# Two heads per block: a chunked linear-attention kernel with a token MLP, rewritten to work on pairs of heads

## The chip, the cores and the metric

The kernel runs on one core of a Trainium2 chip. A core has five engines with instruction streams of their own: PE (matrix products, into the accumulator memory PSUM), DVE (elementwise work, reductions, copies), ACT (functions such as Ln and Exp, and copies), POOL (elementwise work in SBUF, building of constants) and SP, which here only issues transfers. The metric is the time on the device, in microseconds (us). Before the change it is 325.19 us, the median of three runs (324.52 to 325.39).

## The reference

Inputs r, k, v, w have the shape [4 batches, 8 heads, 768 steps, 48]; w lies between 0.80 and 0.95. Each head carries a 48x48 state through the steps:

```python
for t in range(S):
    cur = einsum('bhd,bhe->bhde', u[None] * kt, vt)
    y[:, :, t] = einsum('bhd,bhde->bhe', rt, state + cur)
    state = wt[:, :, :, None] * state + einsum('bhd,bhe->bhde', kt, vt)
```

The heads' outputs are put side by side to x [4, 768, 384]. A token mixer without softmax follows, with weights w_q, w_k [384, 64] and w_out [384, 384]:

```python
W_tok = einsum('bsd,btd->bst', x @ w_q, x @ w_k) / sqrt(64)
out = maximum(einsum('bst,btd->bsd', W_tok, x), 0) @ w_out
```

## The kernel before, in words

Time is cut into 6 chunks of 128 steps. Within a chunk the recurrence becomes matrix products: the running product of w is taken as Exp of a running sum of Ln w (a product with a triangular matrix), r and k are scaled by it (r by the decay up to the step before, k by its inverse), and the chunk's output is a masked 128x128 product A of those two, times v, plus the scaled r times the state. The term with u touches only the diagonal; it is the row sum of u k r times v (VdB).

**Preparation** (lines 116 to 183) loops over the 8 heads of a batch. Four loads of two heads each (k and w on ACT's queue, r and v on SP's, two buffers) feed it. For each head ACT takes Ln (line 135), PE makes two running sums cw0 and cw1 (151, 152), ACT takes Exp of both (156, 157), DVE and POOL scale r and k into one tile, comb (160, 161), PE transposes it (165), DVE and ACT copy the two halves out of PSUM (167, 168), PE makes A in two groups of three chunks (175) and DVE masks it (176). POOL and DVE make the diagonal term (139 to 146). The last row of the decay is taken with products against a unit vector (182) and inverted (183).

**The scan** (185 to 201) loops over the 6 chunks, with all 8 heads in one PSUM tile: Y8 takes for each head AmB times v (128 rows) and r times the state (48 rows), in turn; DVE adds the diagonal term. Sn8 is k times v; DVE adds the state and POOL multiplies by the chunk's decay: the next state.

**The MLP** (203 to 247) transposes X, makes x w_q and x w_k in transposed form, transposes the latter, contracts over time first (Tps, 64x384), then over the 64 (mps, with a Relu), then with w_out (fps), and stores.

All is traced as one straight program. A planner puts each engine's instructions into one order when the kernel is built: it plays the program with its own estimates of cost and gives an engine, whenever it is free, the ready instruction that is earliest in the program text. On the chip each engine then keeps to that order. Tiles come from pools; a tag in a pool has a fixed number of buffers (`bufs`). In PSUM, which has eight banks, tag "big" (Y8, cw0, cw1, psumT) has four buffers and tag "p" (all others) has three:

```python
cw0 = ps.tile([C, NCH, D], F32, name="cw0", tag="big", bufs=4)
A = ps.tile([C, NCH // 2, C], F32, name="A", tag="p", bufs=3)
Y8 = ps.tile([C, H, D], F32, name="Y8", tag="big", bufs=4)
```

All matrix products are issued by a helper at line 52, so the profile shows them under L52 with their tiles' names.

## Time and profile before

| What | Value |
|---|---|
| Median of three runs | 325.19 us |
| Span of the profiled execution | 321.2 us, so about 4 us of a run's time lie outside the span |
| PE busy | 198.6 us, 1,480 products |
| ACT busy | 185.7 us, 290 instructions |
| DVE busy | 130.2 us, 300 instructions |
| POOL busy | 99.8 us, 141 instructions |
| Transfers | 24.3 MB in all, 64 loads of 288 KB and 24 stores of 192 KB |

A row of the groups names line, engine, operation, tiles written and read, shapes and count; then busy time and mean nanoseconds of one, then the idle time of the engine just before them and what ended it. In a row of the timeline come the start, the length and how many instructions of a kind were merged; the lengths of products contain a pipeline's end, so that the distance between starts is the measure of PE's pace. A row of the waits gives who waited for whom, the sum, how often, and the longest. The clock line gives the rate granted to PE in tenths.

### The profile page before, as it was taken

To read this page: it belongs to the slowest core of one execution; us is meant where nothing else is said; L and a number is where in the kernel's file an instruction comes from. 1 tells how busy PE (TensorE), PEld (TensorE's weight loads), DVE (VectorE), ACT (ScalarE), POOL (GpSimd) and SP (SyncE) were. 2 spreads that over 40 slices of the span, in tenths; PEclk is the share of its full clock that TensorE was granted. 3 is DMA by queue.
4 is the path that set the end of the run, shared out by engine and by line. 5 is a ranking of instruction groups with operands and counts; after the bars stand their busy time and mean duration, and the time that the engine had idled before them with its cause. 6 is when DMAs were issued, how large, how long until landed. Compare 5 with 4: busy or idle time off the path is not lost.

```text
span 321.2 us, 4038 instructions
## 1 busy us (share of the span) xinstructions
PE 198.6 (62%) x1480; PEld 126.9 (40%) x1480; DVE 130.2 (41%) x300; ACT 185.7 (58%) x290; POOL 99.8 (31%) x141
## 2 busy tenths in 40 slices
PE   0010453568996654499977654578975643599973
PEld 0000232346662333276642332366642332366631
DVE  0011555355411575563311754454320753653303
ACT  4634688870449978950579786950479574310350
POOL 1344324426311415453303115444303105103200
PEclk9999999999996855555576755555588555555589
DMA  9996454450014397530104762540104250000003
GB/s 154 184 197 130 87 105 82 77 108 2 0 39 73 93 223 127 111 73 2 38 0 76 194 139 44 105 73 2 37 0 76 92 129 1 1 2 2 1 0 147
DMA packets 104006, 24.30 MB, mean 76 GB/s; under 512 B 100529, under 2 KB 103986, under 8 KB 103986
## 3 DMA queue, kind: packets, MB, share of 16 engines
q1 hardware_dynamic: 53522, 14.26, 21.7%
q10 hardware_dynamic: 49664, 9.44, 16.6%
q0 software_dynamic: 800, 0.34, 0.8%
q8 instruction: 11, 0.18, 0.2%
q14 instruction: 9, 0.07, 0.1%
HBM read 19.66 MB, written 4.72 MB: 76 GB/s over the span
## 4 chain that ended last, share of the span: by engine, by line
PE 32%; issue 18%; ACT 17%; POOL 13%; DMA 11%; DVE 6%; SPq 2%; ACTq 0%; POOLq 0%; DVEq 0%
PE Y L52 15%; DMA vG<-in_v_dram 7%; POOL uk L139 4%; POOL urk L143 4%; POOL cbB L161 4%; ACT emcw L157 3%; ACT L156 3%; PE psumT L52 3%; PE wqk_ps L52 3%; ACT Kdc L168 3%; PE xt_ps L52 3%; DMA out_dram<-osb 2%; DVE osb L246 2%; DMA kG<-in_k_dram 2%; PE fps L52 2%
## 5 line engine op out<-in xcount | busy, mean ns | idle before, releaser
L161 POOL TENSOR_TENSOR cbB<-kG,emcw 128x288 bf16<-128x288 f32 x32 | 24.7, 772 | 112.6 <-ACT emcw L157 112.6
L52 PE MATMUL psumT<-ID,cbB 128*128 128x128 bf16 x192 | 25.5, 297 | 50.5 <-POOL cbB L161 38.4
L52 PE MATMUL A<-RdB,Kdc 48*128 48x128 bf16 x192 | 26.5, 298 | 38.6 <-ACT Kdc L168 32.0
L52 PEld LDWEIGHTS <-cbB 128*48 128x48 bf16 (+1 forms) x384 | 26.1, 130 | 58.0 <-POOL cbB L161 53.9
L52 PE MATMUL Y<-SB,RdB 48*128 48x48 bf16 x192 | 41.8, 218 | 3.5 <-POOL SB L200 3.5
L176 DVE TENSOR_TENSOR AmB<-A,US 128x384 bf16<-128x384 f32 x64 | 32.7, 551 | 26.5 <-PE A L52 26.1
L52 PE MATMUL Y<-VbB,AmB 128*128 128x48 bf16 x192 | 41.6, 223 | 0.0
L157 ACT ACTIVATE emcw<-cw,bias_mi 128x288 bf16<-128x288 f32 x32 | 15.9, 498 | 43.0 <-PE cw L52 42.8
L139 POOL TENSOR_TENSOR uk<-kG,ubc 128x288 f32<-128x288 f32 x32 | 25.2, 808 | 45.3 <-DMA kG<-in_k_dram 37.6
L135 ACT ACT_TABLE_LOAD x29 | 37.2, 1283 | 0.5
L52 PEld LDWEIGHTS <-Kdc 48*128 48x128 bf16 x192 | 17.7, 129 | 49.0 <-ACT Kdc L168 41.6
L168 ACT COPY Kdc<-psumT 48x768 bf16<-48x768 bf16 x32 | 25.5, 796 | 12.8 <-DVE RdB L167 12.2
L200 POOL TENSOR_TENSOR SB<-Ss,ptB 48x384 bf16<-48x384 f32 x24 | 20.5, 854 | 35.5 <-DVE Ss L198 35.5
L145 DVE TENSOR_REDUCE diag<-urk 128x6 f32<-128x288 f32 x32 | 14.2, 450 | 39.5 <-POOL urk L143 39.4
L167 DVE COPY RdB<-psumT 48x768 bf16<-48x768 bf16 x32 | 17.4, 544 | 27.4 <-PE psumT L52 27.4
L192 DVE TENSOR_TENSOR X<-Y,VdB 128x384 bf16<-128x384 f32 x24 | 13.3, 555 | 37.4 <-PE Y L52 37.4
L160 DVE TENSOR_TENSOR cbB<-rG,ecwx 128x288 bf16<-128x288 f32 x32 | 15.2, 474 | 30.5 <-ACT ecwx L156 30.0
L156 ACT ACT_TABLE_LOAD x20 | 25.7, 1283 | 1.3 <-ACT logw L135 0.9
L143 POOL TENSOR_TENSOR urk<-uk,rG 128x288 f32<-128x288 f32 x32 | 25.0, 799 | 1.1 <-DMA rG<-in_r_dram 1.0
L52 PEld LDWEIGHTS <-AmB 128*128 128x128 bf16 x192 | 20.1, 107 | 12.5 <-issue 3.9
L208 ACT COPY XT<-xt_ps 128x384 bf16<-128x384 bf16 x24 | 10.3, 483 | 25.1 <-PE xt_ps L52 25.1
L52 PEld LDWEIGHTS <-RdB 48*128 48x128 bf16 x192 | 19.4, 101 | 12.7 <-issue 3.3
(56 smaller groups left out, 283.8 us busy)
## 6 DMA issues: line engine op xcount, KB each, us to landing
kG<-in_k_dram ACTq DMA_DIRECT2D x16, 288.0 KB, 3.9
wG<-in_w_dram ACTq DMA_DIRECT2D x16, 288.0 KB, 4.0
rG<-in_r_dram SPq DMA_DIRECT2D x16, 288.0 KB, 3.6
vG<-in_v_dram SPq DMA_DIRECT2D x16, 288.0 KB, 4.3
out_dram<-osb SPq DMA_DIRECT2D x24, 192.0 KB, 2.0
wout_sb<-in_moe_w_out_dram POOLq DMA_DIRECT2D x1, 288.0 KB, 7.3
wq_f<-in_moe_w_q_dram SPq DMA_DIRECT2D x1, 96.0 KB, 3.8
wk_sb<-in_moe_w_k_dram POOLq DMA_DIRECT2D x1, 48.0 KB, 5.9
```

The lines of the kernel that those rows point to most:

```text
L52: nc.tensor.matmul(o, l, rr, start=start, stop=stop, skip_group_check=sgc, is_transpose=trans)
L135: nc.scalar.activation(logw, wS, ACT.Ln, bias=0.0, scale=LN_SCALE)
L139: nc.gpsimd.tensor_tensor(uk, kS, _rep(ubc[:, ds(h * D, D)], 1, NCH), ALU.mult)
L143: nc.gpsimd.tensor_tensor(urk, uk, rS, ALU.mult)
L156: nc.scalar.activation(ecwx, cw1, ACT.Exp, bias=bias_px, scale=1.0)
L157: nc.scalar.activation(emcw, cw0, ACT.Exp, bias=bias_mi, scale=-1.0)
L160: nc.vector.tensor_tensor(comb[:, :, 0:D], rS, ecwx, ALU.mult)
L161: nc.gpsimd.tensor_tensor(comb[:, :, 64:64 + D], kS, emcw, ALU.mult)
L167: nc.vector.tensor_copy(RdB[:, h], psumT[0:D])
L168: nc.scalar.copy(Kdc, psumT[64:64 + D])
L176: nc.vector.tensor_tensor(AmB[:, h, ds(g * (NCH // 2), NCH // 2)], A, MASKrep, ALU.mult)
L200: nc.gpsimd.tensor_tensor(SB2, Ss, _rep(ptB[:, :, c], 2, D), ALU.mult)
```

## The change

Four things change together.

Heads are worked on in pairs. Tiles with 128 columns hold head one in columns 0 to 47 and head two in columns 64 to 111; the columns between are set to zero once, in standing buffers (three each for logw and Rd, two for Kd and for the decay pt). One transpose then covers two heads, and r and k are transposed apart, both copied out by one DVE instruction (RKT). Exp and the mask work over two PSUM banks at once. A is made per head from partitions 0 to 47 and 64 to 111 of RKT.

The state is kept as one [128, 384] tile. The product of padded k and v of a pair gives a block per head on the diagonal and unwanted blocks beside it; the decay tile pt is zero there, so that the multiplication clears them. The old state is added in PSUM by a product with the identity, and one DVE multiplication makes the new state. The products of r with the state cover two heads each. The last chunk makes no state. The decay comes from products of logw with a column of ones (tile ptp, held over the whole preparation of a batch) and an Exp at its end.

One table set that holds Ln and Exp is named for ACT at the start. All loads are issued on SP's queue, w first, with three buffers; the weights of the MLP are loaded after the first batch's preparation in the text.

In the MLP x w_k is made directly with time on the partitions, two chunks of X are transposed into one PSUM tile, and the Vd product is given to POOL. PSUM is shared out anew: cw, psT and A have one buffer of two banks each, and all other tiles (ptp, Sn, Y8, xt_ps, wkps, wq_ps, Tps, mps, fps) share tag "m" with two buffers of one bank.

The diff, cut to its core (of the lines taken away, most are in the kernel above):

```diff
+    nc.scalar.preload_act_table_set("natural_log_exp_and_others")
...
+    ones = U128[:, C - 1:C]
...
+    nc.gpsimd.memset(bias_c, MU * C)
+    NB = 3
...
+    for i in range(NB):
+        t = consts.tile([C, NCH, C], BF16, name=f"logw{i}", tag=f"logw{i}")
+        nc.gpsimd.memset(t, 0.0)
+        LW.append(t)
+        t = consts.tile([C, NCH, C], BF16, name=f"RdS{i}", tag=f"RdS{i}")
+        nc.gpsimd.memset(t, 0.0)
+        RdS.append(t)
...
+    for i in range(2):
+        t = consts.tile([C, NP, NCH, C], BF16, name=f"KdS{i}", tag=f"KdS{i}")
+        nc.vector.memset(t, 0.0)
+        KdS.append(t)
+        t = consts.tile([C, NCH, H], F32, name=f"pt{i}", tag=f"pt{i}")
+        nc.vector.memset(t, 0.0)
+        PT.append(t)
...
-    ld = ctx.enter_context(tc.tile_pool(name="ld", bufs=2))
+    ld = ctx.enter_context(tc.tile_pool(name="ld", bufs=3))
...
+    def mtile(shape, dtype, name):
+        return ps.tile(shape, dtype, name=name, tag="m", bufs=2)
+
+    def prep(b, hp, AmB, RKT, VB, Vd, ptp):
+        n = b * NP + hp
...
+        for ap, tl in ((w, wG), (k, kG), (r, rG), (v, vG)):
+            nc.sync.dma_start(out=tl, in_=ap[b, ds(hp * 2, 2)].rearrange(
+                "h (c p) d -> p (h c) d", p=C))
+        if n == 0:
+            nc.sync.dma_start(out=u1, in_=u.rearrange("h d -> (h d)"))
+            nc.gpsimd.partition_broadcast(ubc, u1)
...
+        logw = LW[n % NB]
+        for hh in range(2):
+            nc.scalar.activation(logw[:, :, ds(hh * 64, D)],
+                                 wG[:, ds(hh * NCH, NCH)], ACT.Ln,
+                                 bias=0.0, scale=LN_SCALE)
+        cw1 = ps.tile([C, 2, 512], F32, name="cw1", tag="cw")
+        for hh in range(2):
+            mm(cw1[:, hh, 0:NCH * D], US128, logw[:, :, ds(hh * 64, D)])
+        ecwx = hw.tile([C, 2, NCH, D], BF16, name="ecwx", tag="ecwx")
+        nc.scalar.activation(ecwx.rearrange("p h c d -> p h (c d)"),
+                             cw1[:, :, 0:NCH * D], ACT.Exp,
+                             bias=bias_px, scale=1.0)
+        cw0 = ps.tile([C, 2, 512], F32, name="cw0", tag="cw")
...
+        for c in range(NCH):
+            mm(ptp[:, hp, ds(c, 1)], logw[:, c], ones)
+
+        Rd = RdS[n % NB]
+        Kd = KdS[b % 2][:, hp]
+        nc.vector.tensor_tensor(pad(Rd), chd(rG),
+                                ecwx.rearrange("p h c d -> p c h d"), ALU.mult)
+        nc.gpsimd.tensor_tensor(pad(Kd), chd(kG),
+                                emcw.rearrange("p h c d -> p c h d"), ALU.mult)
+        nc.scalar.copy(VB[:, :, ds(hp * 2, 2)], chd(vG))
+
+        psT = ps.tile([C, 2, 1024], BF16, name="psT", tag="psT")
+        for c in range(NCH):
+            mm(psT[:, 0, ds(c * C, C)], Rd[:, c], ID128, trans=True)
+        for c in range(NCH):
+            mm(psT[:, 1, ds(c * C, C)], Kd[:, c], ID128, trans=True)
+        nc.vector.tensor_copy(RKT[:, hp], psT[:, :, 0:NCH * C])
+
+        NG = NCH // 2
+        for g in range(2):
+            A = ps.tile([C, 2, 512], F32, name="A", tag="A")
+            for cc in range(NG):
+                c = g * NG + cc
+                for hh in range(2):
+                    mm(A[:, hh, ds(cc * C, C)],
+                       RKT[ds(hh * 64, D), hp, 1, ds(c * C, C)],
+                       RKT[ds(hh * 64, D), hp, 0, ds(c * C, C)])
+            nc.vector.tensor_tensor(
+                AmB[:, ds(hp * 2, 2), ds(g * NG, NG)],
...
+        nc.gpsimd.tensor_tensor(uk, hcd(kG), _rep(ubs, 2, NCH), ALU.mult)
+        nc.gpsimd.tensor_tensor(uk, uk, hcd(rG), ALU.mult)
+        diag = hw.tile([C, 2, NCH], F32, name="diag", tag="diag")
+        nc.vector.tensor_reduce(diag, uk, axis=AX.X, op=ALU.add)
+        nc.gpsimd.tensor_tensor(Vd[:, :, ds(hp * 2, 2)], VB[:, :, ds(hp * 2, 2)],
+                                _rep(diag.rearrange("p h c -> p c h"), 3, D),
+                                ALU.mult)
 
     for b in range(B):
...
+        ptp = mtile([C, NP, NCH], F32, "ptp")
+        for hp in range(NP):
+            prep(b, hp, AmB, RKT, VB, Vd, ptp)
+        for hh in range(2):
+            nc.scalar.activation(
+                pt.rearrange("p c (q h) -> p q c h", h=2)[ds(hh * 64, D), :, :, hh],
+                ptp[ds(hh * 64, D)], ACT.Exp, bias=bias_c[ds(hh * 64, D)],
+                scale=1.0)
...
+        for c in range(NCH):
+            if c + 1 < NCH:
+                Sn = mtile([C, DM], F32, "Sn")
+                if SB is not None:
+                    mm(Sn, ID128, SB, start=True, stop=False)
+                for hp in range(NP):
+                    mm(Sn[:, ds(hp * D2, D2)], KdS[b % 2][:, hp, c],
+                       VB[:, c, ds(hp * 2, 2)].rearrange("p h d -> p (h d)"),
+                       start=(SB is None and hp == 0), stop=True)
+                SB2 = sm.tile([C, DM], BF16, name="SB2", tag="SB")
+                nc.vector.tensor_tensor(
+                    SB2.rearrange("p (h d) -> p h d", d=D),
+                    Sn.rearrange("p (h d) -> p h d", d=D),
+                    _rep(pt[:, c], 2, D), ALU.mult)
+            Y8 = mtile([C, DM], F32, "Y8")
             for h in range(H):
...
+                mm(Y8[:, ds(h * D, D)], AmB[:, h, c], VB[:, c, h],
+                   start=(h == 0), stop=(c == 0))
+            if SB is not None:
+                for hp in range(NP):
+                    mm(Y8[:, ds(hp * D2, D2)], RKT[:, hp, 0, ds(c * C, C)],
+                       SB[:, ds(hp * D2, D2)], start=False, stop=True)
+            nc.vector.tensor_tensor(X[:, c], Y8,
+                                    Vd[:, c].rearrange("p h d -> p (h d)"), ALU.add)
...
+            if c % 2 == 1:
+                tp = mtile([128, NK, 2 * C], BF16, "xt_ps")
+                for cc in range(2):
+                    for dt in range(NK):
+                        mm(tp[:, dt, ds(cc * C, C)],
+                           X[:, c - 1 + cc, ds(dt * 128, 128)], ID128, trans=True)
+                nc.scalar.copy(XT[:, :, ds((c - 1) * C, 2 * C)], tp)
...
+        wkps = mtile([128, NCH, DH], F32, "wkps")
+        for c in range(NCH):
+            for kt in range(NK):
+                mm(wkps[:, c], XT[:, kt, ds(c * C, C)], wk_sb[:, kt],
+                   start=(c == 0 and kt == 0), stop=(kt == NK - 1))
+        nc.vector.tensor_copy(wk_s, wkps)
...
+        for n in range(2):
+            pp = mtile([DH, 384], F32, "wq_ps")
...
+        Tps = mtile([DH, DM], F32, "Tps")
...
+        for n in range(2):
+            for dt in range(NK):
+                mps = mtile([128, 384], F32, "mps")
...
         for c in range(NCH):
-            fps = ps.tile([128, DM], F32, name="fps", tag="p", bufs=3)
+            fps = mtile([128, DM], F32, "fps")
```

More of the change, by code (lines that the diff above doesn't have):

```diff
@@ L220 @@
[L220 to L229 removed]
+        for n in range(2):
+            pp = mtile([DH, 384], F32, "wq_ps")
+            for kt in range(NK):
+                mm(pp, wq_sb[:, kt], XT[:, kt, ds(n * 384, 384)],
+                   start=(kt == 0), stop=(kt == NK - 1))
+            nc.scalar.copy(wqT[:, ds(n * 384, 384)], pp)
```

170 lines of the change are left out of this document (48 added, 122 removed).

## The prediction

> **What bounds the kernel now.** I read the engines' totals and the granted clock first, then busy time by stage, the chain of waits, the groups by form and, for pitches, the timeline.
>
> ```profile
> span 321.2 us, 4038 instructions
> PE 198.6 (62%) x1480; PEld 126.9 (40%) x1480; DVE 130.2 (41%) x300; ACT 185.7 (58%) x290; POOL 99.8 (31%) x141
> PEclk9999999999996855555576755555588555555589
> ```
>
> No engine is full over the span, so the stages must differ. By stage (start:end, length, then busy time of PE, weight loads, DVE, ACT, POOL, granted clock, DMA share, GB/s):
>
> ```profile
> 40.00:75.00 35.00, 18.23 (x174) 13.19 (x175) 18.68 (x47) 26.76 (x35) 14.63 (x21) 1.00 0.46 86
> 75.00:92.00 17.00, 16.13 (x119) 11.10 (x119) 6.50 (x14) 5.20 (x10) 6.23 (x8) 1.00 0.09 17
> 92.00:112.00 20.00, 14.72 (x71) 7.06 (x69) 6.48 (x14) 17.46 (x29) 4.47 (x6) 0.83 0.29 60
> ```
>
> A batch has three stages. Preparation (40 to 75) is ACT's; the scan over chunks (75 to 92) is PE's, with ACT nearly idle; the token MLP (92 to 112) is ACT's again, because the next preparation runs beside it. From the chain of waits (start, us, what):
>
> ```profile
> 43.20 0.51 ACT emcw L157
> 43.78 0.73 POOL cbB L161
> ...
> 75.60 2.34 PE Y L52 x15
> ...
> 289.52 2.34 PE Y L52 x15
> ```
>
> A hand-over between engines costs about 0.07 us (43.71 to 43.78). The first scan is in full flow at 75.6, the fourth at 289.5: the period is 213.9/3 = 71.3 us, and 31.7 follow. The span is 75.6 + 3 x 71.3 + 31.7, and I forecast these three terms.
>
> **The change, engine by engine.** A "pair" is the two heads that the new preparation works on together; a batch has four.
>
> ```profile
> L135 ACT ACT_TABLE_LOAD x29 | 37.2, 1283 | 0.5
> L156 ACT ACT_TABLE_LOAD x20 | 25.7, 1283 | 1.3 <-ACT logw L135 0.9
> L157 ACT ACT_TABLE_LOAD x9 | 11.5, 1283 | 4.4 <-PE cw L52 4.3
> L157 ACT ACTIVATE emcw<-cw,bias_mi 128x288 bf16<-128x288 f32 x32 | 15.9, 498 | 43.0 <-PE cw L52 42.8
> L135 ACT ACTIVATE logw<-wG 128x288 bf16<-128x288 f32 x32 | 14.0, 442 | 1.3 <-DMA wG<-in_w_dram 0.9
> L168 ACT COPY Kdc<-psumT 48x768 bf16<-48x768 bf16 x32 | 25.5, 796 | 12.8 <-DVE RdB L167 12.2
> L161 POOL TENSOR_TENSOR cbB<-kG,emcw 128x288 bf16<-128x288 f32 x32 | 24.7, 772 | 112.6 <-ACT emcw L157 112.6
> L200 POOL TENSOR_TENSOR SB<-Ss,ptB 48x384 bf16<-48x384 f32 x24 | 20.5, 854 | 35.5 <-DVE Ss L198 35.5
> L114 POOL MEMSET SB<- 48x384 bf16 x4 | 1.7, 418 | 0.0
> L176 DVE TENSOR_TENSOR AmB<-A,US 128x384 bf16<-128x384 f32 x64 | 32.7, 551 | 26.5 <-PE A L52 26.1
> L145 DVE TENSOR_REDUCE diag<-urk 128x6 f32<-128x288 f32 x32 | 14.2, 450 | 39.5 <-POOL urk L143 39.4
> L167 DVE COPY RdB<-psumT 48x768 bf16<-48x768 bf16 x32 | 17.4, 544 | 27.4 <-PE psumT L52 27.4
> ```
>
> **ACT.** 58 table loads cost 74.4 us. One set for Ln and Exp removes them, and Kdc's 25.5 us moves into DVE's joint copy. From 288 to 768 elements ACT adds 298 ns, 0.62 an element, so one Exp over two banks and 576 elements is 0.50 + 0.18 = 0.68 us (at worst two old ones, 1.00). A pair: two Ln 0.88, two Exp 1.36, the V copy 0.62, together 2.9 us; with some 7 us of evacuations a batch is 19 against 46 now.
>
> **DVE.** 288 and 384 elements give 148 ns plus 1.05 an element. A pair: Rd 0.75, joint copy of 1,536 bf16 0.94 (the old copy's 0.52 an element), two masks of 768 at 0.95, reduction 0.75: 4.35 us. Some 18 evacuations of 0.55 in scan and MLP add 10: 27 us a batch. The Vd product moves to POOL.
>
> **POOL.** Kd, uk, uk times r, and now Vd, each over 576 elements. Upper bound twice 772, 1.54; lower, by the step from 288 to 384 elements (82 ns for 96), 1.02. I take 1.45, near the same operation on the same 128 partitions: 5.8 us a pair, 23 a batch; the scan's loop loses its SB product. The six new memsets of 768 elements, 0.4 to 0.8 us each, lie while the first loads are under way; uncovered they would cost at most 4.8 once.
>
> ```profile
> 35.38 0.82 PE L52 MATMUL psumT<-ID,cbB 128*128 128x128 bf16 x6
> 36.00 0.45 PE L52 MATMUL cw<-logw,U 128*128 128x288 bf16 x1
> 36.24 0.45 PE L52 MATMUL cw<-logw,US 128*128 128x288 bf16 x1
> 70.94 0.26 PE L52 MATMUL Y<-VbB,AmB 128*128 128x48 bf16 x2
> 75.88 0.22 PE L52 MATMUL Y<-SB,RdB 48*128 48x48 bf16 x1
> 76.03 0.22 PE L52 MATMUL Y<-VbB,AmB 128*128 128x48 bf16 x1
> 77.87 0.51 PE L52 MATMUL Sn<-VbB,cbB 128*48 128x48 bf16 x8
> 110.48 0.29 PE L52 MATMUL cw<-logw,U 128*128 128x288 bf16 x1
> 110.60 0.29 PE L52 MATMUL cw<-logw,US 128*128 128x288 bf16 x1
> ```
>
> **PE.** Starts 0.24 us apart for 288 columns are 0.83 ns a column; at 110 us they are 0.12 apart. So the early stages run at half rate, though the clock line says 9 there. Eight Sn in 0.51 are about 0.043 each, their 48 columns; two AmB products in a row 0.04, so a 128x128 weight load doesn't show. But AmB (128 rows) alternating with RdB (48 rows) starts every 0.15, and these are the chunk's 2.34 us. The change groups them, both on 128 rows. A chunk is then identity 384 columns, Sn 4x96, Y 8x48 + 4x96, transposes 384: 1,920, 1.6 us. A pair: 4x288 for cw, 12x128 transposes, 12x128 for A: 3.5 us (2.9 if the two row halves of A overlap, which no row shows; I take 3.5, psumT's pitch). The MLP: 18x64 + three times 2,304 + 18x384 = 14,976 columns, 12.4 us at half rate, 6.2 at full. A batch: 14 + 9 + 12.4, some 36 us at half rate.
>
> On the weight loads one page speaks against padding 48 columns to 128: the Trainium skill, "TensorE: Matmul & The Clock Gate", section LDWEIGHTS, gives a load its columns over 1.2 GHz, 107 ns for 128 against 40 for 48. Its section on Fast Weight Load makes full 128-column loads faster, and the two AmB products agree with that. A batch by the first is rival 3.
>
> **Who holds which buffer.** Nine kinds of PSUM tile now share the two buffers of tag m; cw, psT and A have one buffer each. How a tag hands out buffers shows in the first batch's MLP. These are rows of the timeline and of the waits:
>
> ```profile
> 94.22 0.80 ACT L168 COPY Kdc<-psumT 48x768 bf16<-48x768 bf16 x1
> 111.75 0.32 PE L52 MATMUL A<-RdB,Kdc 48*128 48x128 bf16 x3 [0.86 <-DVE osb L246]
> PE A L52 <- DVE osb L246: 3.7, 4, 1.3
> ```
>
> A of the next batch has its operand at 95.0 and starts at 111.75, released by osb, although it shares three buffers of tag p with an MLP that seldom needs all. So a tag gives buffers out in the order of the program text, and what is later in the text waits even when ready. In the new kernel ptp of batch b+1 then waits until the MLP of b has placed its last fps. Its products read logw, whose three standing buffers rotate, so the Ln of a batch's fourth pair waits for them. Three pairs are prepared beside scan and MLP; the fourth lies bare behind the MLP: ptp 0.3, Ln 0.9, cw 0.7, Exp 0.7, cw 0.7, Exp 0.7, Kd 1.45, transposes 0.85, copy 0.95, twice A 0.85 and mask 0.95: 10.9, plus 13 hand-overs 0.9, less 0.8 beside the last fps: 11 us. Its uk, Vd and V copy don't need logw and are done earlier. Behind the waiting Ln the whole preparation of that pair is late, and through Kd and AmB the next scan.
>
> **Loads.** All go to SP's queue. In the stage 28 to 30 us ACT had issued no load since 18.4, and SP's queue alone moved 186 GB/s:
>
> ```profile
> 18.43 0.37 ACTq L123 DMA_DIRECT2D wG<-in_w_dram  x1
> 33.88 0.37 ACTq L123 DMA_DIRECT2D kG<-in_k_dram  x1
> 28.00:30.00 2.00, 0.00 (x0) 0.00 (x0) 0.00 (x0) 0.66 (x2) 0.00 (x0) 1.00 0.95 186
> rG<-in_r_dram SPq DMA_DIRECT2D x16, 288.0 KB, 3.6
> ```
>
> So a 288 KB load takes 1.6 us in a stream, 64 of them 102 us in all: covered by three buffers and the long periods. Stores share SP's queue, as before.
>
> **The sum.** First term: w lands at 4 (issue plus 3.6); Ln, cw, Exp, cw, Exp and hand-overs bring POOL's first Kd to 8.4; three pairs at 5.8, the broadcast of u 0.7 and 2 of waiting for diag bring the fourth Kd to 28.5 (its w lands at 4 + 12 x 1.6 = 23, so the loads don't bound it); Kd and the five steps to the last mask, 7.2 with hand-overs: 36 us (34 to 37 over POOL's bounds) against 75.6.
>
> Period: the loop of a chunk is identity and Sn 0.64, drain 0.2, DVE 0.55, hand-over: 1.5, with Y and transposes in its shadow, but 1.6 to PE and more to two buffers: two Sn and two Y tiles live about 1.4 each and xt 1.6, 7.2 over two buffers, 1.8 a chunk. With waits for xt and ends, 14 us for a scan alone; with three pairs' PE and DVE instructions of up to 0.95 in between, 18. MLP: PE 12.4 at half rate, 9 at a clock like 0.83, plus drains between its five steps and 0.55 at the end: 15. So 18 + 15 + 11 = 44. End: scan alone 14, MLP 15, last store and finish 2: 31. Span 36 + 132 + 31 = 199. The median lies 4 over the profiled span (325.2 to 321.2): 203 us. Own range 190 to 220: the clock in the MLP alone is worth 4 x 6 us, POOL's bounds and the Exp's some 6 together.
>
> **Rivals.**
> 1. The fourth pair is hidden too: the three buffers of logw or tag m don't hold it back, and the period is PE's 36. 36 + 108 + 31 + 4 = 179. For it: nothing else is over 27. Against: the A row.
> 2. Buffers are given to whoever is ready: ptp of b+1 takes one early and keeps it through scan and MLP. Each tile then runs alone: a chunk 1.4 + 1.4 + 0.8, plus DVE's other work 1.2, 4.8; the MLP 28. Period 57, total 36 + 171 + 31 + 4 = 242. Against: the same row.
> 3. A 128-column weight load shows at psumT's pitch, 0.10: ptp, Y and the MLP's 18 small products rise, a batch is 16.6 + 14 + 13.4 = 44 of PE, and with the bare 11 a period of 55: 36 + 165 + 33 + 4 = 238. Against: AmB's 0.04.
> 4. The one set doesn't hold, two loads a pair stay: 2.6 in each bare pair and 10 of ACT a batch, some 20 in all: 223. Nothing in this trace can exclude it.
> 5. Slower than before: the single queue moves strided loads much more slowly once it alone has 64 of them. Behind the last load lie 12 of preparation and 31, so it decides from (325 - 47)/64 = 4.3 us a load, 68 GB/s. Against: 186.
>
> **How the numbers follow.** Chances: forecast 0.50, rival 1 0.22, 2 0.09, 3 0.10, 4 0.04, 5 0.05. I predict 203. Range 172 to 242, rival 1 with a full-rate PE at its foot and rivals 2 to 4 at its top, leaving out under 0.1. A difference of 0.3% is what runs of this kernel can tell from none; faster 0.94, same 0.01, slower 0.05.
>
> **What would show it.** ACT has one or two table loads; Y products start 0.04 to 0.08 apart without 0.15; ptp runs behind fps, and a PE gap of some 11 us follows each MLP; SP's loads land at 1.6 us pitch; the first Y block is done near 37. If preparation is continuous across the MLP, rival 1 holds; if Sn waits on X at every chunk and a batch takes 57, rival 2. The forecast fails if POOL needs over 2 us an operation or scan instructions queue behind preparation on PE.

## The result and the profile after

The changed kernel takes 182.78 us (median of four runs, 181.64 to 183.93) against 325.29 for the kernel before on the same chip (four runs, 324.52 to 327.02): a ratio of 0.5605, 95% interval 0.5574 to 0.5637. The forecast was 203, with a range of 172 to 242. The time lies in the range, but below the 190 to 220 that the likeliest case had for itself. Some executions of a kernel come out some per cent slower; two of e2's four below and one of e5's two did, and the figures for these two kernels go by the others.

The profiled execution has a span of 182.1. First the head of its page: span, the engines' totals, the granted clock and the DMA share in 40 slices.

```profile
span 182.1 us, 3121 instructions
...
PE 121.0 (66%) x1200; PEld 74.3 (41%) x1200; DVE 112.7 (62%) x156; ACT 74.0 (41%) x140; POOL 95.3 (52%) x86
...
PEclk9999999999999997585599999657999697557969
DMA  7999999999999300399999908999940240000024
```

ACT has gone from 185.7 to 74.0 us and PE from 198.6 to 121.0. No engine is full over the span, so the stages are read again: the first batch's preparation, then scan, MLP and bare stretch of the first batch, the second scan, and the last scan (start:end, length, then busy time of PE, weight loads, DVE, ACT, POOL, granted clock, DMA share, GB/s).

```profile
0.00:53.00 53.00, 20.43 (x172) 12.90 (x172) 26.77 (x27) 18.34 (x35) 34.95 (x42) 1.00 1.24 178
53.00:63.40 10.40, 8.13 (x133) 6.09 (x132) 10.40 (x18) 5.30 (x9) 8.77 (x7) 1.00 0.94 132
63.40:78.40 15.00, 12.59 (x87) 5.96 (x85) 10.78 (x16) 5.29 (x11) 8.77 (x7) 0.77 0.18 58
78.40:89.90 11.50, 8.96 (x90) 6.02 (x90) 5.49 (x8) 6.96 (x14) 6.09 (x5) 0.61 1.11 210
89.90:99.70 9.80, 8.11 (x129) 5.99 (x128) 9.80 (x17) 5.52 (x9) 6.51 (x5) 0.93 1.16 186
158.00:168.00 10.00, 8.27 (x100) 6.22 (x101) 4.51 (x9) 2.40 (x3) 0.00 (x0) 0.58 0.01 2
```

The first term is still the longest single piece. A scan with preparation beside it takes 10 us, in which DVE is busy without a break (10.40 of 10.40, 9.80 of 9.80); the MLP takes 15; then follow 11.5 us in which DVE falls to half (5.49 of 11.50). The marks between these stages are the first Y products in full flow and, one us behind, the first X on DVE (timeline of PE, then of DVE):

```profile
52.99 0.58 PE L54 MATMUL Y<-VB,AmB 128*128 128x48 bf16 x10
```

```profile
53.98 1.01 DVE L250 TENSOR_TENSOR X<-Y,Vd 128x384 bf16<-128x384 f32 x2
...
90.77 1.01 DVE L250 TENSOR_TENSOR X<-Y,Vd 128x384 bf16<-128x384 f32 x2
...
157.60 1.01 DVE L250 TENSOR_TENSOR X<-Y,Vd 128x384 bf16<-128x384 f32 x2
```

By the prediction's own sum the span is 53.0 + 3 x 34.5 + 25.5 = 182.1, where 34.5 is (157.60 - 53.98)/3. Forecast were 36, 44 and 31. So the first term is 17 longer, the periods 3 x 9.5 shorter and the end 5.5 shorter: three errors, of which one hid behind the other two.

The groups that answer to the prediction's prices:

```profile
L168 POOL TENSOR_TENSOR KdS<-kG,emcw 128x576 bf16<-128x576 f32 x16 | 22.2, 1388 | 41.5 <-ACT emcw L158 33.2 <-issue 7.0 <-DMA rG<-in_r_dram 1.2
L166 DVE TENSOR_TENSOR RdS<-rG,ecwx 128x576 bf16<-128x576 f32 x16 | 20.8, 1298 | 20.2 <-ACT ecwx L151 14.6 <-DMA rG<-in_r_dram 5.6
...
L199 POOL TENSOR_TENSOR Vd<-VB,diag 128x576 bf16<-128x576 bf16 x16 | 18.7, 1172 | 8.4 <-ACT VB L170 6.2 <-DVE diag L198 2.2
...
L151 ACT ACTIVATE ecwx<-cw,bias_px 128x576 bf16<-128x576 f32 x16 | 11.9, 741 | 24.6 <-PE cw L54 24.5
...
L57 ACT ACT_TABLE_LOAD x1 | 1.3, 1283 | 0.7 <-PEq L312 0.7
```

One table load; Exp 0.74 (forecast 0.68). POOL's four are 1.39 for Kd and 1.17 for Vd, with 1.50 and 1.48 on the same page for the two uk products: 5.5 a pair (four at 1.45, 5.8, were forecast). One row stands out: RdS takes 1,298 ns on the mean where 0.75 was reckoned.

### The profile page after: what moved, and what is told of

The parts are those of the page before. It is cut to its first block, busy times and chain, and to the rows that moved or that the text cites. A ratio compares the mean times of both kernels' runs of the same rounds, so it can differ in the third digit from the quotient of the medians.

```text
span 182.1 us, 3121 instructions
## 1 busy us (share of the span) xinstructions
PE 121.0 (66%) x1200; PEld 74.3 (41%) x1200; DVE 112.7 (62%) x156; ACT 74.0 (41%) x140; POOL 95.3 (52%) x86
## 4 chain that ended last, share of the span: by engine, by line
PE 25%; DVE 23%; issue 18%; POOL 12%; ACT 7%; DMA 7%; SPq 6%; POOLq 1%; ACTq 0%; DVEq 0%
DVE RdS L166 6%; PE psT L54 6%; DVE X L250 5%; SPq L127 5%; DVE RKT L177 5%; POOL uk L196 4%; DMA wG<-in_w_dram 3%; ACT XT L260 3%; POOL uk L195 3%; PE cw L54 3%; POOL Vd L199 3%; PE wq_ps L54 2%; PE fps L54 2%; DVE AmB L188 2%; PE Tps L54 2%
## 5 line engine op out<-in xcount | busy, mean ns | idle before, releaser
L168 POOL TENSOR_TENSOR KdS<-kG,emcw 128x576 bf16<-128x576 f32 x16 | 22.2, 1388 | 41.5 <-ACT emcw L158 33.2
L188 DVE TENSOR_TENSOR AmB<-A,US 128x768 bf16<-128x768 f32 x32 | 30.4, 950 | 5.7 <-PE A L54 4.4
L166 DVE TENSOR_TENSOR RdS<-rG,ecwx 128x576 bf16<-128x576 f32 x16 | 20.8, 1298 | 20.2 <-ACT ecwx L151 14.6
L177 DVE COPY RKT<-psT 128x1536 bf16<-128x1536 bf16 x16 | 15.3, 953 | 19.4 <-PE psT L54 19.3
L195 POOL TENSOR_TENSOR uk<-kG,ubc 128x576 f32<-128x576 f32 x16 | 24.0, 1499 | 0.0
L196 POOL TENSOR_TENSOR uk<-uk,rG 128x576 f32<-128x576 f32 x16 | 23.6, 1476 | 0.6
L199 POOL TENSOR_TENSOR Vd<-VB,diag 128x576 bf16<-128x576 bf16 x16 | 18.7, 1172 | 8.4 <-ACT VB L170 6.2
L54 PE MATMUL A<-RKT 48*128 48x128 bf16 x192 | 17.5, 263 | 7.0 <-DVE RKT L177 4.2
L144 ACT ACTIVATE logw<-wG 128x288 bf16<-128x288 f32 x32 | 12.4, 435 | 23.7 <-PE ptp L54 11.3
L151 ACT ACTIVATE ecwx<-cw,bias_px 128x576 bf16<-128x576 f32 x16 | 11.9, 741 | 24.6 <-PE cw L54 24.5
L54 PEld LDWEIGHTS <-KdS 128*128 128x128 bf16 x176 | 16.1, 123 | 13.7 <-POOL KdS L168 9.9
L54 PE MATMUL fps<-wout_sb,mixT 128*128 128x384 bf16 x72 | 19.7, 418 | 1.7 <-ACT mixT L288 1.2
L54 PE MATMUL cw<-logw,US 128*128 128x288 bf16 x32 | 10.5, 365 | 13.4 <-ACT logw L144 12.9
```

The lines of the kernel that those rows point to most:

```text
L54: nc.tensor.matmul(o, l, rr, start=start, stop=stop, skip_group_check=sgc, is_transpose=trans)
L144: nc.scalar.activation(logw[:, :, ds(hh * 64, D)], wG[:, ds(hh * NCH, NCH)], ACT.Ln, bias=0.0, scale=LN_SCALE)
L151: nc.scalar.activation(ecwx.rearrange("p h c d -> p h (c d)"), cw1[:, :, 0:NCH * D], ACT.Exp, bias=bias_px, scale=1.0)
L166: nc.vector.tensor_tensor(pad(Rd), chd(rG), ecwx.rearrange("p h c d -> p c h d"), ALU.mult)
L168: nc.gpsimd.tensor_tensor(pad(Kd), chd(kG), emcw.rearrange("p h c d -> p c h d"), ALU.mult)
L177: nc.vector.tensor_copy(RKT[:, hp], psT[:, :, 0:NCH * C])
```

## Where the first term went

Two stops are in the first 53 us. The first is on POOL (timeline; the bracket gives the idle time ahead and what ended it):

```profile
12.74 0.68 POOL L131 PARTITION_BROADCAST ubc<-u  x1 [6.12 <-issue]
20.43 1.77 POOL L168 TENSOR_TENSOR KdS<-kG,emcw 128x576 bf16<-128x576 f32 x1 [7.01 <-issue]
```

Between the last memset and the broadcast of u lie 6.12 us, between the broadcast and the first Kd 7.01, and the profile names nothing that POOL waited for ("issue"). The forecast had POOL's first Kd at 8.4, and it starts at 20.43, 12 us late. ACT's part in that is 3.6: its first emcw is done at 11.98, since its order has the V copy, which waits 3.90 us for v, ahead of the first Exp. The other 8.4 are POOL's. By the fourth Kd (forecast 28.5, measured 35.82) 7.3 of it are left. The Trainium skill, "GPSIMD Engine Reference", section 2.1, says that the first call to a freshly loaded custom routine pays a code load of about 6 us which no instruction of the profile shows. If the broadcast is such a routine, the gap ahead of it agrees with that size, but some 2.5 us of the gap can be the load of u itself, issued at 5.03 behind a load of v that landed at 9.1. Of the 7 us behind the broadcast, ahead of an ordinary elementwise operation, the Trainium skill says nothing.

The kernel before has the same broadcast, and its rows stood in the trace from which the forecast was made (timeline of POOL, before):

```profile
9.48 0.68 POOL L81 PARTITION_BROADCAST ubc<-u  x1 [7.18 <-issue]
...
20.30 0.78 POOL L139 TENSOR_TENSOR uk<-kG,ubc 128x288 f32<-128x288 f32 x1 [7.61 <-DMA wG<-in_w_dram]
```

There the second stop bears the name of a load of w, which this product doesn't read. The forecast took from these rows the 0.68 and not the idle time.

The second stop is the long RdS of the fourth pair (timelines of DVE and of POOL at that time):

```profile
38.77 6.48 DVE L166 TENSOR_TENSOR RdS<-rG,ecwx 128x576 bf16<-128x576 f32 x1
```

```profile
38.41 1.17 POOL L199 TENSOR_TENSOR Vd<-VB,diag 128x576 bf16<-128x576 bf16 x1
...
43.25 1.39 POOL L195 TENSOR_TENSOR uk<-kG,ubc 128x576 f32<-128x576 f32 x1
44.71 1.80 POOL L196 TENSOR_TENSOR uk<-uk,rG 128x576 f32<-128x576 f32 x1
```

POOL has five instructions in a row without a gap, from 38.41 to 44.64; RdS, issued at 38.77 with both operands in SBUF, ends at 45.25, just after POOL's first gap (44.64 to 44.71). It needs 0.75 alone, and it stood behind POOL for the other 5.7. What stands behind it on DVE is late by as much. The Trainium skill, "SBUF — State Buffer", section Who interferes with whom, has the rule: a DVE instruction with two SBUF inputs contends with a GpSimd instruction that reads SBUF. The Trainium skill speaks there of an exclusive lock on the ports that the two share. The trace agrees with the contention. The Trainium skill gives no length for such a wait; here it went through a whole run of POOL instructions, 5.7 us.

Such a long wait came once in the changed kernel. In three other places RdS got its turn after one POOL instruction, without a gap in POOL's order, and POOL's next one took longer instead, 1.91 where 1.4 is usual. One of them (timeline of DVE, then of POOL):

```profile
63.05 1.40 DVE L166 TENSOR_TENSOR RdS<-rG,ecwx 128x576 bf16<-128x576 f32 x1
```

```profile
63.80 1.91 POOL L195 TENSOR_TENSOR uk<-kG,ubc 128x576 f32<-128x576 f32 x1
```

What decides between the two, no run here separates.

## The experiments

Each is timed beside the kernel before on its own chip, and the ratios below go by that. The table gives, from the profiled execution of each variant of the changed kernel, the start of the first X, the three distances from there to the next batch's first X, and what follows the last.

| Kernel | Median, us | Ratio to before (95%) | First X | Periods | Rest |
|---|---|---|---|---|---|
| after | 182.78 | 0.5605 (0.5574 to 0.5637) | 54.0 | 36.8, 34.4, 32.5 | 24.5 |
| e1 u by a load | 180.81 | 0.5571 (0.5536 to 0.5606) | 45.5 | 38.0, 36.5, 35.4 | 25.0 |
| e2 four logw | 175.51 | 0.5402 (0.5360 to 0.5444) | 56.2 | 26.3, 32.2, 34.5 | 24.9 |
| e3 both | 179.51 | 0.5535 (0.5487 to 0.5583) | 42.3 | 36.6, 37.3, 34.5 | 27.0 |
| e4 no diagonal | 166.45 | 0.5123 (0.5077 to 0.5169) | 43.7 | 32.7, 33.5, 31.7 | 23.7 |
| e5 no set chosen | 197.83 (one run) | | 54.4 | 44.8, 39.7, 33.5 | 23.7 |
| e8 stores on ACT | 184.09 | 0.5672 (0.5621 to 0.5723) | 53.9 | 38.1, 34.2, 32.1 | 24.3 |
| e9 Y interleaved | 182.94 | 0.5639 (0.5604 to 0.5675) | 53.8 | 36.8, 35.9, 30.8 | 24.5 |
| e10 Rd from PSUM | 188.50 | 0.5808 (0.5779 to 0.5836) | 51.2 | 37.2, 37.6, 36.9 | 24.3 |
| e11 both, stores late | 183.05 | 0.5640 (0.5616 to 0.5664) | 42.2 | 36.3, 37.9, 38.8 | 26.2 |
| e12 loads run ahead | 167.54 | 0.5174 (0.5137 to 0.5212) | 49.6 | 28.1, 31.3, 32.5 | 24.0 |

### The first term: e1, e4, e10

e1 brings u to all partitions by a load and drops POOL's broadcast.

```diff
-            nc.sync.dma_start(out=u1, in_=u.rearrange("h d -> (h d)"))
-            nc.gpsimd.partition_broadcast(ubc, u1)
+            nc.sync.dma_start(out=ubc, in_=_rep(u.rearrange("h d -> (h d)"), 0, C))
```

> The changed kernel with u spread over the partitions by the load itself instead of POOL's partition broadcast. In the changed kernel POOL's first elementwise instruction starts at 20.43 us after 7.0 us of idleness that no row explains, although its operand emcw is there at 12.0. Theory: the broadcast costs POOL a hidden stop of some 6 us before and 7 us after it. Then the first POOL product starts near 12 to 13, the first scan comes 7 to 8 us earlier and the kernel takes about 175 us. Rival: the idle time is a wait for a load or another engine that the profile doesn't name; then the start stays near 20 and the time within 1 us of 182.8.

POOL's timeline in e1:

```profile
10.42 1.81 POOL L194 TENSOR_TENSOR uk<-kG,ubc 128x576 f32<-128x576 f32 x1 [4.12 <-DMA ubc<-in_u_dram]
```

POOL starts at 10.42 instead of 20.43 and waits for a named transfer; both unnamed stops are gone with the broadcast. So the broadcast is what they hang on. The first X comes 8.5 us earlier, but the median falls by 2 only, and the intervals of the two ratios overlap, since each period is 1 to 3 longer: the time is given back later (below, e3). RdS is blocked here too, 5.07 us from 16.39, until POOL stops at 20.79 to issue a transfer of its own.

e4 leaves the diagonal term out, that is, three of POOL's four instructions a pair and one of DVE's.

```diff
+    Vd = consts.tile([C, NCH, H, D], BF16, tag="Vd")
+    nc.vector.memset(Vd, 0.0)
...
-        nc.gpsimd.tensor_tensor(uk, hcd(kG), _rep(ubs, 2, NCH), ALU.mult)
-        nc.gpsimd.tensor_tensor(uk, uk, hcd(rG), ALU.mult)
...
-        nc.vector.tensor_reduce(diag, uk, axis=AX.X, op=ALU.add)
-        nc.gpsimd.tensor_tensor(Vd[:, :, ds(hp * 2, 2)], VB[:, :, ds(hp * 2, 2)],
```

> The changed kernel without the diagonal term: uk, its product with r, its row sum and the Vd product are left out, Vd is a tile of zeros, so the output lacks u's part. POOL keeps only Kd. In the changed kernel DVE's RdS product at 38.77 lasts 6.48 us, until the first gap in POOL's unbroken run of instructions (37.05 to 44.65), where others last 0.76. Theory: a DVE instruction with two operands in SBUF stands still while POOL reads without a gap. Then all sixteen RdS last about 0.76 and the first scan comes 6 us and more earlier; with POOL's own backlog gone as well, about 165 us. Rival: the long RdS is a wait for r's load that the record counts as work; then one or more long RdS stay.

The view of one tile gives least, median and greatest duration in ns; here is RdS in e4:

```profile
L168 DVE TENSOR_TENSOR RdS<-rG,ecwx x16: 748/758/1691, 10.4 to 134.0; 128x576 bf16<-128x576 f32 x16
```

The greatest falls from 6,481 to 1,691, with the same operands and the same DVE instruction. POOL still starts its first Kd at 21.3, and yet the first X comes 10.3 earlier: with POOL free the late start costs little. The 16 us include the work that was left out and say nothing of what moving it would bring.

e10 gives Rd an operand in PSUM: the first Exp is written back into cw1.

```diff
-        ecwx = hw.tile([C, 2, NCH, D], BF16, name="ecwx", tag="ecwx")
-        nc.scalar.activation(ecwx.rearrange("p h c d -> p h (c d)"),
-                             cw1[:, :, 0:NCH * D], ACT.Exp,
-                             bias=bias_px, scale=1.0)
+        ecwx = cw1[:, :, 0:NCH * D]
+        nc.scalar.activation(ecwx, ecwx, ACT.Exp, bias=bias_px, scale=1.0)
```

> The changed kernel with the first Exp of a pair written back into its own PSUM tile cw, so that DVE's Rd product reads one operand from SBUF (rG) and one from PSUM. If Rd stands still because two SBUF inputs contend with POOL's, every Rd now takes under 1.2 us, the one of 6.5 us is gone, and the first term falls by about 5; against that the second cw product waits for Rd, one DVE instruction of 0.8 us with a hand-over more in each bare stretch: 175 to 181 us. Rival: DVE stands still behind POOL whatever it reads, the long Rd stays and the time is 183 to 188.

RdS in e10, and below it from the waits of e10 the price:

```profile
L164 DVE TENSOR_TENSOR RdS<-rG,cw x16: 744/745/755, 10.3 to 154.4; 128x576 bf16<-128x576 f32 x16
```

```profile
PE cw L54 <- DVE RdS L164: 9.8, 3, 5.5
```

All 16 take 744 to 755 ns. Three of them meet POOL at work; the clearest is the fourth pair's, inside a run of POOL instructions without a gap (timelines of DVE and of POOL in e10):

```profile
37.34 0.74 DVE L164 TENSOR_TENSOR RdS<-rG,cw 128x576 bf16<-128x576 f32 x1
```

```profile
36.54 1.42 POOL L193 TENSOR_TENSOR uk<-kG,ubc 128x576 f32<-128x576 f32 x1
37.90 1.19 POOL L197 TENSOR_TENSOR Vd<-VB,diag 128x576 bf16<-128x576 bf16 x1
```

So Rd stands still for its second SBUF operand, not for DVE or its order: the mechanism is shown. The time went the wrong way all the same. cw has one buffer, the second cw product now waits for Rd (9.8 us in three places), and the periods grow from 36.8, 34.4, 32.5 to 37.2, 37.6, 36.9. My expectation had the gain at 5 and the loss at one instruction of 0.8 us and a hand-over a period; the gain in the first X was 2.8 and the loss some 8.

### The bare stretch: e2

Four logw and RdS buffers instead of three, so that the fourth pair need not wait for the first pair's decay products.

```diff
-    NB = 3
+    NB = 4
```

In the changed kernel the forecast chain is there, in the waits and in ACT's timeline:

```profile
ACT logw L144 <- PE ptp L54: 11.3, 2, 6.0
...
PE ptp L54 <- DVE osb L296: 2.7, 3, 1.4
```

```profile
78.81 1.11 ACT L144 ACTIVATE logw<-wG 128x288 bf16<-128x288 f32 x3 [7.12 <-issue]
```

Ln of the waiting pairs runs 0.4 us into the stretch, behind ptp, which is behind the MLP's last fps.

> The changed kernel with four standing logw and Rd buffers instead of three. Theory: the bare stretch of 11 us behind each MLP (78.4 to 89.9, 112.8 to 124, 147.8 to 158) stands there because the Ln of a batch's fourth pair waits for ptp products that read the oldest logw; with a fourth buffer that pair is prepared beside the MLP too. Three stretches shrink from 11 to 2 or 3 us, but loads (29 us of transfers a batch), DVE (28) and POOL then set a period of 28 to 30 instead of 34.5: about 165 us. Rival: the stretch belongs to tag m alone, whose buffers ptp gets late whatever logw does, so that the scan waits all the same: 180 us or more.

The first batch's end and the second's beginning in e2, on DVE:

```profile
79.98 1.01 DVE L296 COPY osb<-fps 128x384 f32<-128x384 f32 x2
...
82.48 0.56 DVE L250 TENSOR_TENSOR X<-Y,Vd 128x384 bf16<-128x384 f32 x1
```

From the MLP's last evacuation to the next first X it is 2.5 us; in the changed kernel it was 12.9 (77.83 to 90.77). So the three buffers did hold the fourth pair back, as forecast (the edit gives RdS a fourth buffer too; the waits above are those of logw). The first period falls by 10.5. But the later two do not keep it (32.2 and 34.5 against 34.4 and 32.5), and the time falls by 7.3, not by the 18 expected.

### Why two gains do not add: e3, e11, e8

e3 has both edits.

> Both edits together: u by load, four logw and Rd buffers. If the two stops are separate places, the gains add, 8 and 18 us: about 157 us. If loads are the next bound (64 at 1.6 us with stores between them, until about 125 us, and 35 to 40 us of work behind the last one), the sum stops near 160 to 165.

The time is 179.51, not 157 to 165, and by the ratios slower than e2 alone. The first X comes at 42.3, 12 us early, and the periods are 36.6, 37.3 and 34.5. My next theory was SP's queue. In e3 it issues no load from 49.1 to 66.9; the r and v of the second batch's fourth pair stand behind stores that wait for the MLP. In the changed kernel that queue waited 66.4 us in 19 places for osb. Two runs test it. e8 moves the changed kernel's stores to ACT's queue:

```diff
-            nc.sync.dma_start(out=out[b, ds(c * C, C), :], in_=osb)
+            nc.scalar.dma_start(out=out[b, ds(c * C, C), :], in_=osb)
```

> The changed kernel with its 24 output stores issued by ScalarE and not by SyncE; all loads stay on SyncE. In the profile of the changed kernel SyncE's queue waits 66.4 us in 19 places for osb, that is, loads of the next batch stand behind stores that wait for the MLP's end: no load is issued between 60.3 and 73.1 us. If these late loads cost time, they do so after the bare stretch, where the pairs after it wait for v, k and w: 3 to 8 us less, 175 to 180 us. Rival: the three buffers of a load tag hold the loads back anyway, and the time stays within 1% of 182.8. Third possibility: the stores now hold up ScalarE's own Ln and Exp behind osb, and the time rises by up to 5 us.

No gain: 184.09 against 182.78, and the intervals of the two ratios overlap. So in the changed kernel the stores on SP's queue cost nothing, or what they cost came back: in the waits of e8 ACT's Ln now stands behind the stores on ACT's own queue.

```profile
ACT logw L144 <- DMA out_dram<-osb: 14.4, 3, 6.5
```

e11 leaves the stores on SP, but writes those of a batch behind the next batch's preparation, on top of e3.

```diff
             prep(b, hp, AmB, RKT, VB, Vd, ptp)
+        for c, t in late:
+            nc.sync.dma_start(out=out[b - 1, ds(c * C, C), :], in_=t)
+        late = []
...
-            nc.sync.dma_start(out=out[b, ds(c * C, C), :], in_=osb)
+            if b + 1 < B:
+                late.append((c, osb))
+            else:
+                nc.sync.dma_start(out=out[b, ds(c * C, C), :], in_=osb)
```

> Experiment e3 (u by a load, four logw buffers) with one edit more: the stores of a batch are written in the program after the preparation of the next batch, with six osb buffers, so that on SyncE's queue all loads of that preparation stand ahead of the stores and not behind them. In e3 no load was issued from 49 to 67 us and r and v of the second batch's fourth pair followed at 66.9 and 70.9, behind stores. If that is what took e3's gain, the bare stretch shrinks to some 3 us in each of three periods: 177.7 - 3 x 5 to 8, 155 to 165 us. Rival: the gain was lost to PE or DVE being shared out otherwise, and the time stays at 177 to 181.

The queue did what was wanted: the fourth pair's r and v are issued at 49.1 and 50.6. Yet the first period is 36.3, and the theory falls. What ACT does at that time in e11:

```profile
52.31 0.80 ACT L263 COPY XT<-xt_ps 128x768 bf16<-128x768 bf16 x1 [5.14 <-PE xt_ps L54]
...
59.80 0.47 ACT L278 CAST wqT<-wq_ps 64x384 bf16<-64x384 f32 x1 [0.74 <-PE wq_ps L54]
60.17 0.77 ACT L143 ACTIVATE logw<-wG 128x288 bf16<-128x288 f32 x2
...
64.14 1.38 ACT L291 ACTIVATE mixT<-mps 128x384 bf16<-128x384 f32 x3
...
65.97 0.78 ACT L143 ACTIVATE logw<-wG 128x288 bf16<-128x288 f32 x2
```

ACT stands idle for 5.14 us ahead of an XT copy, although the load of w for the next pair had been issued at 39.7; that third pair's Ln (60.17) comes behind wqT, the fourth pair's (65.97) behind the last Relu, both without idle time of their own. ACT keeps to the order it was built with, and in that order the third pair lies behind wqT and the fourth behind the last Relu. In e2, where the first X comes 14 us later, the Ln of all four pairs of the second batch lies ahead of the MLP's wqT in that order, and the fourth pair's Ln runs at 64.51, no later than e3's at 64.62. So an earlier first scan came without an earlier preparation of the second batch, and the wait moved from the first term to the first period. That the order is what costs it is read from these rows; no run moved those two Ln alone. Why e11's third period is 4.3 longer than e3's stays open.

### One more step: e12

e2 with four buffers for each load, and stores written behind the preparation of the batch after next, so that loads can run two batches ahead.

```diff
-    ld = ctx.enter_context(tc.tile_pool(name="ld", bufs=3))
+    ld = ctx.enter_context(tc.tile_pool(name="ld", bufs=4))
...
-    mout = ctx.enter_context(tc.tile_pool(name="mout", bufs=4))
+    mout = ctx.enter_context(tc.tile_pool(name="mout", bufs=12))
...
+        while late and (late[0][0] < b - 1 or b + 1 == B):
+            lb, c, t = late.pop(0)
+            nc.sync.dma_start(out=out[lb, ds(c * C, C), :], in_=t)
```

> Experiment e2 (four logw and RdS buffers) with the loads freed: four buffers a load tag, and the stores of a batch written in the program after the preparation of the batch after next (twelve osb buffers), so that on SyncE's queue no load of the next two batches stands behind them. In e2 the queue issued no load from 63.9 to 77.9 us, and ScalarE then waited 8.1 us for w and 10.0 for v. If the loads behind stores cost time, these waits go and each of the second and third periods falls from 30 to 26 to 28: 174 - 5 to 10 in the span, 167 to 172 us in the median. Rival: what bounds the periods is PE and the order of the instructions on ScalarE, as e11 suggests, and the time stays within 1.5% of 177.

167.54 us: the time came out as expected, the reason only in part. The DMA line of e12's page is full without a break to the 27th of 40 slices, some 112 us, and the last load is issued by 107.7; the changed kernel's line above has three holes:

```profile
DMA  6999999999999999999999999992000250000034
```

But the second and third periods are 31.3 and 32.5, not 26 to 28, 3.0 us less than in e2 together, and the first period is 1.8 longer. The largest part, 6.6 us, came in the first term, where I had expected nothing. Its fourth RdS, on DVE and against POOL:

```profile
40.63 1.17 DVE L166 TENSOR_TENSOR RdS<-rG,ecwx 128x576 bf16<-128x576 f32 x1
```

```profile
40.64 0.81 POOL L226 DMA_DIRECT2D wout_sb<-in_moe_w_out_dram  x1
```

With other edits POOL's order came out otherwise: the weight's transfer, 0.81 us in which POOL computes nothing, stands where RdS waits, and RdS takes 1.17 instead of the 6.28 that it took in e2. e12 is the fastest kernel of the case that does all the work, 8% under the changed one; of the 8 us by which it is below e2, the 6.6 in the first term are luck of the order.

### The parts of the change: e5, e6, e7, e9

e5 is the changed kernel without the first line, e6 the kernel before with it.

```diff
-    nc.scalar.preload_act_table_set("natural_log_exp_and_others")
```

> The changed kernel without its first line, which loads the one table set for Ln and Exp ahead of everything. If the choice of the set does the work, the switches come back: two loads a pair of 1.28 us (the duration in the profile before), 32 or more in all, some 41 us more busy time on ScalarE. ScalarE is busy 4.2 of every 10 us in the changed kernel, so much of that is hidden; what shows is the load in each of the four bare stretches of one pair and in the first term: 10 to 20 us, 193 to 203 us (rival 4 of the prediction priced it at 20). The rival, that the compiler finds the common set by itself, gives one load and 182 to 184 us.

> The kernel before with one part of the change alone: the one table set for Ln and Exp is loaded ahead of everything. ScalarE's 58 loads (74.4 us) fall to one. Preparation is ScalarE's in the kernel before (26.8 of 35 us busy in the stage from 40 to 75, a good third of it loads), so if the stage falls to what DVE and PE need (18.7 and 18.2 of 35) each of four batches loses 10 to 15 us: 260 to 285 us. Rival: the chain Ln, cw, Exp, cw, Exp of one head is bound by its hand-overs, and the loads only fill its waits: over 300 us.

The groups of e5:

```profile
L143 ACT ACT_TABLE_LOAD x16 | 20.5, 1283 | 8.8 <-issue 6.7 <-DMA wG<-in_w_dram 1.8
...
L150 ACT ACT_TABLE_LOAD x13 | 16.7, 1283 | 0.2
```

With three more at line 157, 32 loads, two a pair, 41 us of ACT, and 197.83 against 182.78: 15 us, where rival 4 had 20. This rests on one run. In the kernel before the set alone gives 304.96 (ratio 0.9392, 0.9292 to 0.9491). ACT's 185.7 us fall to 107.7 there, but the time by only 20: the rival that the loads mostly fill waits of a chain was right, and my 260 to 285 was wrong. A quarter of the busy time taken off ACT came through.

e7 is the kernel before with the Y products of a chunk grouped by operand, e9 the changed kernel with its Y products taken in turn.

```diff
-                mm(Y8[:, h], AmB[:, h, c], VbB[:, h, c], start=True, stop=False,
+                mm(Y8[:, h], AmB[:, h, c], VbB[:, h, c], start=(h == 0), stop=False,
...
+            for h in range(H):
```

> The kernel before with one part alone: in each chunk all eight Y products on AmB (128 rows) come first, then the eight on RdB (48 rows), so that the row count changes twice a chunk and not 16 times. If the alternation costs the 0.15 us from start to start that the profile before shows, 16 products take about 0.9 us and not 2.34, five chunks of a batch lose some 7 us where the scan lies alone on PE (17 us a batch): 4 x 4 to 7 us, 297 to 309 us. Rival: another wait in the chunk's loop (DVE's Ss, POOL's SB) sets its 2.8 us, and the time stays within 1% of 325.

```diff
-            if SB is not None:
-                for hp in range(NP):
+                if SB is not None and h % 2 == 1:
+                    hp = h // 2
```

> The changed kernel with the Y products of a chunk in another order: two on AmB, then the one on RKT of the same pair, and so on, all of them on 128 rows. If it is the change of the row count that costs 0.15 us, the products still start 0.04 to 0.09 us apart and the time stays within 1% of 182.8. If any alternation between two kinds of operand costs it, each of 8 switches a chunk adds 0.1: 0.8 us in each of 20 chunks, 16 us, 190 to 199.

PE's timeline in e7 and in e9 (the first pair of numbers behind the names is the standing operand, rows by columns):

```profile
71.44 0.50 PE L52 MATMUL Y<-VbB,AmB 128*128 128x48 bf16 x8
71.88 0.50 PE L52 MATMUL Y<-SB,RdB 48*128 48x48 bf16 x8
72.31 0.51 PE L52 MATMUL Sn<-VbB,cbB 128*48 128x48 bf16 x8
72.75 0.22 PE L52 MATMUL Y<-VbB,AmB 128*128 128x48 bf16 x1
```

```profile
53.00 0.28 PE L54 MATMUL Y<-VB,AmB 128*128 128x48 bf16 x2
53.10 0.23 PE L54 MATMUL Y<-SB,RKT 128*128 128x96 bf16 x1
```

In e7 sixteen products take 0.87 us (71.44 to 72.31) where they took 2.34, and the time is 294.58 (ratio 0.9072, 0.9002 to 0.9142): 30 us from an order alone, about 20 chunks by 1.5. That is more than the 16 to 28 I gave it, because it lay on the path: from its first X to its last, a scan takes 8.9 to 10.6 us where it took 15.8 to 17.6. In e9 products on AmB and RKT alternate, all on 128 rows, and go on starting 0.05 us apart; the time is unchanged. So alternation between operands of the same shape is free, and what cost 0.1 us a product in the kernel before is the change of the row count between 128 and 48. Rows are not the only shape that counts. Between the last Sn and the next AmB product of e7, both on 128 rows and without a wait, the columns of the standing operand change from 48 to 128, and the starts are 0.14 apart:

```profile
72.61 0.21 PE L52 MATMUL Sn<-VbB,cbB 128*48 128x48 bf16 x1
72.75 0.22 PE L52 MATMUL Y<-VbB,AmB 128*128 128x48 bf16 x1
```

e7 also sets the flag that opens a sum in PSUM at the first product of a block alone. That isn't the cause: from its eighth AmB product to its first RdB product the flag is the same, and the starts are 0.15 apart (71.73 and 71.88). The other parts of the change (work in pairs, the state in one tile, one queue for the loads) were not timed alone.

## Why the prediction was right or wrong

**The three-term sum** held as a way of reckoning, and the path: scan, MLP and bare stretch follow each other in every period. The total was inside the range because the errors had different signs, and that was luck.

**First term, 36 forecast, 53.0 measured.** The failed step is "Ln, cw, Exp, cw, Exp and hand-overs bring POOL's first Kd to 8.4", which gave the broadcast of u its 0.7 us of work and nothing else (the 7.2 and 7.6 us of idle time beside it in the trace before were left out), and which had no V copy waiting for v ahead of the Exp; and with it the price of Rd, 0.75, taken from an instruction with nobody beside it. The late start left 7.3 us at the fourth Kd. Of the other 9.7 the block is 5.7; the last 4 are mostly order by the timelines: Kd ends at 37.11, but Rd stands on DVE behind a mask and is issued at 38.77; the mask that the first chunk's last Y products need ends at 51.07, but PE starts them at 52.99, behind the next pair's transposes. No run took these apart. e1 removed the late start, e4 and e10 the block.

**Period, 44 forecast, 34.5 measured.** Bare stretch 11 forecast, 11.5 measured, by the mechanism forecast: ptp behind osb, Ln behind ptp, Ln at the stretch's beginning. MLP 15 forecast, 13 to 15 measured. The scan failed: 18 forecast, 10 measured. Six chunks take 1.6 us each even in the last scan, alone and at a granted clock of 0.58, so the "14 us for a scan alone" was 4 too much, with its waits for xt and ends; and the 4 added for instructions of preparation in between are not there, as PE had room (8.13 of 10.40 at a clock of 1.00). DVE is what fills the scan.

**End, 31 forecast, 25.5 measured**: the same 4 of the scan; MLP, last store and finish take 15.5 together instead of 17.

**Half rate.** I costed PE at half rate through scan and MLP, 36 us a batch. The granted clock was 0.93 to 1.00 in the scans with preparation beside them and 0.77, 1.00 and 0.87 in the first three MLPs; PE's busy time is 121 us, 30 a batch.

**What would show it.** One table load, Y starts 0.04 us apart (ten products in 0.41), ptp behind fps, 178 GB/s of loads over the first 53 us: seen. The PE gap of some 11 us behind each MLP was not: PE is busy 8.96 of the 11.50 us of the first bare stretch, because it works there on the waiting pair, on the next batch's first pair and on the first products of the scan. "The first Y block is done near 37" failed too, and it pointed at the right term.

**Rivals.** Rival 1 (179 us) is the nearest number and was the wrong mechanism: the fourth pair is bare, and e2 shows what hiding it brings. Rival 2's period of 57 did not come, nor rival 3's pitch of 0.10. Rival 4's condition did not come; brought about in e5, it cost 15 where 20 was its price. Rival 5 had 4.3 us a load as its point; the loads took 1.5 to 1.6.

## What to carry to other kernels

Price an elementwise instruction on DVE by what POOL does beside it: with two SBUF operands it can wait for one POOL instruction or for a whole run of them, and an operand in PSUM takes the wait away (here at a higher price than the wait). When a period is a sum of stages, an earlier start is worth something only if the next batch's preparation starts earlier too; look on each in-order engine for what that preparation stands behind. Before pairing or padding anything, group products by the shape of their standing operand: that alone took 30 us off the kernel before. And read the idle time beside a row as well as its length: the stops beside the broadcast stood in the trace before.

## What the runs showed of the hardware

- DVE's Rd, 0.75 us alone, took 6.48 behind five POOL instructions in a row, until a gap of 0.07 us in POOL's order; in other places it waited for one POOL instruction and took 1.05 to 1.40. With one operand in PSUM all 16 took 0.744 to 0.755.
- Around one partition broadcast of 0.68 us POOL stood still for 6.1 us ahead and 7.0 behind, under no name but "issue"; with u brought by a load both stops were gone.
- Products whose standing operand changes between 128 and 48 rows, or between 48 and 128 columns, start 0.14 to 0.15 us apart; on one shape 0.06 or less, whether operands alternate or not.
- 32 table loads of 1.28 us cost 15 us of the changed kernel's time (one run), and 58 of them 20 of the time before: of 41 and 74 us of loads, a third and a quarter came through.
